# Fourier filter and two spectral MLP layers, float32: three tables of due steps and one choice of transposer are changed

## The chip, the cores and the metric

The kernel runs on one core of a Trainium2 chip. The metric is the device time of one execution in microseconds (us). TensorE is called PE in the rows (PEld is its weight load), VectorE DVE, ScalarE ACT, GpSimd POOL, and SyncE SP; SP only issues DMAs.

## The reference

Three layers follow each other on x of shape (4, 3136, 256), in float32. The first filters along the sequence; the other two are MLPs of width 1024, each behind a normalisation of its rows.

```python
def _attn_ref(x, filt_r, filt_i):
    X = np.fft.rfft(x, axis=1)
    return np.fft.irfft(X * (filt_r + 1j * filt_i)[None], n=x.shape[1], axis=1)

def _moe_ref(x, w_ch1, w_ch2):
    u = x + np.real(np.fft.fft(np.fft.fft(x, axis=1), axis=2))
    un = (u - mu(u)) / np.sqrt(var(u) + 1e-06)
    return u + np.maximum(un @ w_ch1, 0.0) @ w_ch2

def _moe2_ref(x, g_ln, w_ch1, w_ch2):
    xn = (x - mu(x)) / np.sqrt(var(x) + 1e-06) * g_ln
    return x + np.maximum(xn @ w_ch1, 0.0) @ w_ch2
```

## The kernel before

The sequence of 3136 = 64 x 49 is transformed as a two-dimensional DFT made of matmuls. For each of the four batches a first pass (`over_p`, a generator) goes over the factor 64 and a second (`over_q`) over the factor 49; the results go through DRAM. The rest works on 24 full **units** of 512 tokens (four tiles of 128), six for each batch, and on unit 24, the border of all batches, which has two tiles.

A unit is first prepared (`prep_ticks`: the mixing matmuls that make its tokens `u`, then its normalisation), then goes through the first MLP layer (`layer` 0, weights w1a and w2a) and later through the second (`layer` 1, w1b and w2b). Every layer of a unit is a block of eight **steps** m = 0 to 7, one for each 128 of the 1024 hidden columns. The blocks stand in the order (0,0), (1,0), (0,1), (2,0), (1,1), (3,0), and so on. With s the step at which block (U, 0) begins, (U-1, 1) begins at s+8, (U+1, 0) at s+16 and (U, 1) at s+24.

Each matrix product is done in three passes of a split operand, high times high, low times high and high times low, where high is the rounded value and low the remainder. A step is therefore `w1_step` (six matmuls `ps<-xth,w1` and `ps<-xtl,w1`, 512 columns each, line 766), `w1_evict` (ACT writes `hh`, line 776, then DVE writes `hl`, line 777) and `w2_step` (twelve matmuls of 256 columns, line 794). The main loop runs the first product two steps ahead:

```python
        for i, (U, layer, m) in enumerate(steps):
            if i + 2 < len(steps):
                w1_step(*steps[i + 2])
            for f in at.pop(i, []):
                f()
            if i in conv_at:
                run(cw, 1)
            w2_step(U, layer, m)
            if i + 2 < len(steps):
                w1_evict(*steps[i + 2])
```

All other work is cut into ticks (what a generator does up to its next `yield`), and tables of numbers say at which step, counted from s, each tick is issued (`at`). There is no scheduler: each engine runs its instructions in the order in which this program issues them. In a step an engine has the ticks first and the eviction of the hidden columns behind them.

The normalisation (`ln_ticks`) comes in two forms.
- For the blocks in the set `TURN` the tokens are turned without PE: a tick with the statistics (DVE, and a power on POOL), two ticks in which ACT writes two normalised tiles each (`xn`, line 654), a tick with a 32 x 32 transpose on DVE (line 668) and a DMA to DRAM (`xd`, line 670), a tick with four DMAs that bring it back turned (`xtl<-xd`, line 679), and two ticks that split it into `xth` (ACT, line 688 in layer 0 and 684 in layer 1) and `xtl` (DVE, lines 689 and 685).
- For the others a tick holds the statistics, the next the normalised tiles on DVE (line 663), and two ticks each transpose one half by PE (line 695) and split it from PSUM (lines 223 and 224 in layer 0, 697 and 698 in layer 1).

The pool of `xn` has one buffer. The second form is used in layer 0 by the first unit of each batch (6, 12, 18) and by the border unit 24. The title's "border unit" is any of these four: units that PE turns while the unit before them, U = 5, 11, 17 and 23, waits for its second layer. Their ticks are due at `PREPN`, s + 3, 3, 5, 7, 8, 9, 11, 13; the two PE transposes are the ticks at s+11 and s+13. The second layer of U has its ticks at `LNT`, s + 10, 11, 12, 13, 16, 19, 20, where the ticks at s+11 and s+12 write `xn`. In units whose layer 0 is in `TURN` the preparation has its ticks at `PREPT`.

The two passes of the next batches are ticks too. `over_p` lies over the end of a batch (around U = 5 and 11) and adds three matmuls of 512 columns to a step (line 220), an eviction (`gst`, line 370), an operand split on ACT and POOL (`sh`, `sl`, lines 223 and 224) and a load on SP (`xr<-in_x`, line 258). `over_q` lies over the other units of batches 0 to 2. From U = 17 on nothing but preparation and MLP is left.

Of the kernel before, what the change touches and what calls it, by code (L numbers as in the profile page):

```python
# [28 lines left out]
NU = 6 * B  # L29
# [108 lines left out]
OPQ = (2, 4)  # L138
MID = 16
PAIRS = [(4, 5), (10, 11), (0, 1), (2, 3), (12, 14), (6, 8)]  # L140
TURN = {(U, l) for U in range(3, NU) for l in range(2) if l or U % 6}
PREPT = (0, 1, 3, 4, 5, 6, 7, 8, 10, 13, 13)
LNT = (10, 11, 12, 13, 16, 19, 20)
PREP1 = (0, 1, 2, 3, 3, 4, 5, 5)
PREPS = (2, 3, 5, 8, 8, 9, 11, 11)
PREPN = (3, 3, 5, 7, 8, 9, 11, 13)
LN0 = (8, 10, 12, 12)
LN = (12, 13, 16, 19)
# [3 lines left out]
def spectral_mlp_kernel(ctx: ExitStack, tc, x, ff, cst, w1a, w2a, gln, w1b, w2b, out):  # L152
# [73 lines left out]
    def split_tiles(src, lo_eng=None):  # L226
        n = src.shape[0]
        h = spl.tile([128, 512], F32R, tag="h", name="sh")
        l = spl.tile([128, 512], F32R, tag="l", name="sl")
        w = 1  # L230
        for s in src.shape[1:]:
            w *= s
        flat = src.rearrange("p a d -> p (a d)") if len(src.shape) == 3 else src
        split(flat, h[:n, :w], l[:n, :w], lo_eng)
        return {"h": h, "l": l}
# [324 lines left out]
    def prep_ticks(U):  # L560
# [15 lines left out]
        if U:  # L576
            vs = [split_tiles(t, e) for t, e in zip(v_raw.pop(U), (nc.gpsimd, nc.gpsimd if (U, 0) in TURN else nc.vector))]
        else:
# [47 lines left out]
    def ln_ticks(U, layer, sets=None):  # L626
        n = tiles(U)
        u = u_of[U]
        xs = {}
        turn = (U, layer) in TURN  # L630
        xall = None
# [180 lines left out]
    with tc.manual_schedule():  # L812
# [98 lines left out]
        def put(s, it, k=1):  # L911
            at.setdefault(s, []).append(lambda: run(it, k))

        def call(s, f, *a):
            at.setdefault(s, []).append(lambda: f(*a))
# [5 lines left out]
        for U in range(NU + 1):  # L921
            s = index[U, 0]
            V = U + 1
            if V <= NU:
                it = prep_ticks(V)
                ws = PREPT if (V, 0) in TURN else (PREPS if V % 6 else PREPN) if U else PREP1
                for w in ws:
                    put(s + w, it)
                new = V % 6 == 0 and V < NU
                call((s - 3 if (V, 0) in TURN else s + 1 + new) if U else -1, load_v, V)  # L930
                if new:
                    ready[V // 6] = s + 2
            it = ln_ticks(U, 1)
            if U < NU:
                e = index[U + 1, 0]
                for w in [s + v for v in (LNT if (U, 1) in TURN else LN)] if U else [e - 8 + w for w in LN0]:
                    put(w, it)
            else:
                for w in (9, 10, 12, 13):
                    put(s + w, it)  # L940
# [54 lines left out]
def _launch(inputs):  # L995
# [44 lines left out]
    with tile.TileContext(nc) as tc:  # L1040
        spectral_mlp_kernel(tc, *args)
# [22 lines left out]
```

## Time and profile before

| | before |
|---|---|
| median of 3 runs | 1401.95 us (1398.85 to 1402.89) |
| profiled execution, its own time | 1401.71 us |
| span of its instructions | 1399.9 us, mean granted TensorE clock 0.992 |
| PE busy / weight load | 1358.1 us (97%) / 1198.6 us (86%) |
| DVE / ACT / POOL busy | 879.5 us (63%) / 748.2 us (53%) / 436.2 us (31%) |

The span runs from the first to the last instruction of the profiled execution; 1.8 us of its time lie around it. Times of rows are counted from the start of the span. PE is busy almost throughout, so time is lost where PE stands still, where its clock is lower, or where it is given more matmuls; the other engines matter where PE waits for them. A matmul's end is modelled and reaches past the start of the next, so PE's pace is read from the starts.

### The profile page before, as it was taken

The numbers are of one execution on the slowest core, as the hardware profiler recorded it, in microseconds if no ns is written. First come the engines' busy times: TensorE is split into PE (matmuls) and PEld (weight loads), VectorE is DVE, ScalarE is ACT, GpSimd is POOL, SyncE is SP. The second block draws the span as 40 slices with busy tenths as digits, with TensorE's granted clock in tenths as the row PEclk, the third lists the DMA queues.
The fourth block names the chain that finished last, engine by engine and source line by source line (L and its number), as shares of the span: only waits on it lengthen the run. The fifth ranks groups of instructions, "written<-read, shape, count | busy, mean of one in ns | idle before, by whom it ended". The sixth has DMA issues, their size and how long they took to land.

```text
span 1399.9 us, 23346 instructions
## 1 busy us (share of the span) xinstructions
PE 1358.1 (97%) x8611; PEld 1198.6 (86%) x8611; DVE 879.5 (63%) x1719; ACT 748.2 (53%) x1533; POOL 436.2 (31%) x379
## 2 busy tenths in 40 slices
PE   8979899999999999999999999999999999999988
PEld 6547798888888989898888998898898999999978
DVE  5978877777544766767444667677554554555433
ACT  5665555665535565756445656566534444454232
POOL 1746444544222333524033244344111101110000
PEclk9999999999999999999999999999999999999999
DMA  8872324363524634624525544444222413331210
GB/s 298 283 231 86 98 85 114 123 174 87 147 91 138 153 84 135 184 61 116 132 76 145 145 125 141 123 125 121 64 46 61 91 31 76 76 87 35 61 46 23
DMA packets 228642, 158.11 MB, mean 113 GB/s; under 512 B 168528, under 2 KB 192080, under 8 KB 228528
## 3 DMA queue, kind: packets, MB, share of 16 engines
q1 hardware_dynamic: 212576, 133.41, 34.9%
q10 hardware_dynamic: 15952, 23.20, 5.2%
q8 instruction: 68, 1.11, 0.3%
q14 instruction: 46, 0.38, 0.1%
HBM read 100.35 MB, written 56.23 MB: 112 GB/s over the span
## 4 chain that ended last, share of the span: by engine, by line
PE 85%; DVE 4%; ACT 4%; issue 2%; DMA 2%; SPq 1%; POOL 1%; ACTq 0%; DVEq 0%; POOLq 0%
PE ps L794 35%; PE ps L766 35%; PE ps L220 8%; PE ps L591 2%; ACT xn L654 2%; PE ps L308 1%; PE ps L325 1%; PE ps L478 1%; ACT hh L776 1%; DMA xr<-in_x 1%; DVE hl L777 1%; PE ps L446 1%; DVE wm L748 1%; DMA ww<-in_w2a 0%; PE ps L341 0%
## 5 line engine op out<-in xcount | busy, mean ns | idle before, releaser
L777 DVE SCALAR_TENSOR_TENSOR hl<-ps,hh 128x512 fp32r<-128x512 f32 (+1 forms) x400 | 270.2, 676 | 332.3 <-ACT hh L776 323.0
L776 ACT ACTIVATE hh<-ps 128x512 fp32r<-128x512 f32 (+1 forms) x400 | 234.1, 585 | 328.4 <-PE ps L794 318.5
L766 PE MATMUL ps<-xth,w1a 128*128 128x512 f32 (+1 forms) x800 | 247.0, 390 | 1.0 <-ACT xth L688 0.3
L766 PE MATMUL ps<-xth,w1b 128*128 128x512 f32 (+1 forms) x800 | 244.7, 388 | 0.0
L794 PEld LDWEIGHTS ps<-w2b,hh 128*128 128x128 f32 x1568 | 210.1, 190 | 24.7 <-ACT hh L776 11.6
L794 PE MATMUL ps<-w2b,hh 128*128 128x256 f32 x1568 | 218.8, 282 | 10.3 <-ACT hh L776 10.3
L794 PE MATMUL ps<-w2a,hh 128*128 128x256 f32 x1568 | 218.0, 281 | 3.7 <-ACT hh L776 3.3
L794 PEld LDWEIGHTS ps<-w2a,hh 128*128 128x128 f32 x1568 | 207.6, 189 | 15.5 <-ACT hh L776 4.1
L654 ACT ACTIVATE xn<-u,nb,rs 128x256 f32<-128x256 f32 x156 | 123.1, 838 | 70.3 <-DVE nb L647 47.4
L766 PE MATMUL ps<-xtl,w1a 128*128 128x512 f32 (+1 forms) x400 | 157.5, 394 | 1.8 <-DVE xtl L689 1.4
L766 PE MATMUL ps<-xtl,w1b 128*128 128x512 f32 (+1 forms) x400 | 156.2, 391 | 0.0
L643 POOL TENSOR_TENSOR rs<-rs,mhalf 128x4 f32<-128x4 f32 (+1 forms) x51 | 50.7, 994 | 334.0 <-DVE rs L642 220.5
L766 PEld LDWEIGHTS ps<-xth,w1a 128*128 128x128 f32 x800 | 136.9, 190 | 19.4 <-ACT xth L688 1.9
L766 PEld LDWEIGHTS ps<-xth,w1b 128*128 128x128 f32 x800 | 135.6, 188 | 16.7
L461 POOL TENSOR_TENSOR y<-y,t 128x512 f32<-128x512 f32 (+1 forms) x67 | 94.4, 1409 | 146.4 <-DVE t L459 113.8
L794 PE MATMUL ps<-w2a,hl 128*128 128x256 f32 x784 | 122.8, 278 | 4.0 <-DVE hl L777 3.9
L794 PE MATMUL ps<-w2b,hl 128*128 128x256 f32 x784 | 123.3, 279 | 0.0
L794 PEld LDWEIGHTS ps<-w2a,hl 128*128 128x128 f32 x784 | 104.4, 189 | 4.6 <-DVE hl L777 4.6
L224 POOL TENSOR_TENSOR sl<-gr,sh 98x512 fp32r<-98x512 f32 x48 | 62.2, 1295 | 146.3 <-ACT sh L223 146.3
L794 PEld LDWEIGHTS ps<-w2b,hl 128*128 128x128 f32 x784 | 105.1, 190 | 0.0
L798 DVE TENSOR_TENSOR u<-ps,u 128x512 f32<-128x512 f32 x98 | 63.2, 686 | 52.9 <-PE ps L794 52.9
L766 PEld LDWEIGHTS ps<-xtl,w1a 128*128 128x128 f32 x400 | 75.6, 189 | 20.6 <-DVE xtl L689 4.8
(130 smaller groups left out, 2074.8 us busy)
## 6 DMA issues: line engine op xcount, KB each, us to landing
fc<-in_ff SPq DMA_DIRECT2D x61, 512.0 KB
xd<-xn SPq DMA_DIRECT2D x39, 512.0 KB
xtl<-xd SPq DMA_DIRECT2D x156, 128.0 KB
vd<-vst ACTq DMA_DIRECT2D x64, 200.0 KB
xr<-in_x SPq DMA_DIRECT2D x48, 256.0 KB
vr<-vd SPq DMA_DIRECT2D x48, 256.0 KB
out<-u SPq DMA_DIRECT2D x24, 512.0 KB
gr<-gd SPq DMA_DIRECT2D x48, 196.0 KB
```

Source lines behind the costliest of these rows:

```text
L220: nc.tensor.matmul(out=o, lhsT=lhs[a], rhs=rhs[b], start=start and i == 0, stop=stop and i == 2)
L224: (lo_eng or nc.vector).tensor_tensor(out=lo, in0=src, in1=f32(hi), op=ALU.subtract)
L308: nc.tensor.matmul(out=o, lhsT=cf[i // 512][:k, i % 512:i % 512 + w], rhs=rhs[:k, c0:c1], start=start, stop=stop)
L461: (nc.gpsimd if b or t < n - 1 else nc.vector).tensor_tensor(out=y[:, :nk], in0=y[:, :nk], in1=t2[:, :nk], op=ALU.add)
L591: nc.tensor.matmul(out=o, lhsT=lhs, rhs=rhs[r], start=i == 0, stop=False)
L643: nc.gpsimd.tensor_tensor(out=rs[:, tl], in0=rs[:, tl], in1=mhalf[:, tl], op=ALU.pow)
L654: nc.scalar.activation(out=xs[t], in_=u[:, t].rearrange("p (k a j) -> p j k a", k=2, j=4), func=ACTF.Identity, scale=rs[:, t:t + 1], bias= ...
L766: nc.tensor.matmul(out=o, lhsT=w[:, a, k, m * 128:m * 128 + 128], rhs=xt[s][:, k, :n], start=i == 0, stop=i == 5)
L776: nc.scalar.activation(out=h[:, :n], in_=ps[:, :n], func=ACTF.Relu)
L777: nc.vector.scalar_tensor_tensor(out=l[:, :n], in0=ps[:, :n], scalar=0.0, in1=f32(h[:, :n]), op0=ALU.max, op1=ALU.subtract)
L794: nc.tensor.matmul(out=o[:, t % 2], lhsT=a[:, t * 128:t * 128 + 128], rhs=w[:, b, m], start=m == 0 and i == 0 and t % 2 == 0, stop=m == 7 ...
L798: nc.vector.tensor_tensor(out=u[:, t - 1:t + 1], in0=o, in1=u[:, t - 1:t + 1], op=ALU.add)
```

## The change

Four edits of the tables, lines 141 to 144 and 936 of the new kernel. Lines after 143 stand one lower in the new kernel (766 becomes 767).

```diff
-TURN = {(U, l) for U in range(3, NU) for l in range(2) if l or U % 6}
-PREPT = (0, 1, 3, 4, 5, 6, 7, 8, 10, 13, 13)
+TURN = {(U, l) for U in range(3, NU) for l in range(2) if (U < NU - 1 if l else U % 6)}
+PREPT = (0, 1, 3, 4, 5, 6, 7, 8, 10, 12, 12)
 LNT = (10, 11, 12, 13, 16, 19, 20)
+LNTN = (11, 14, 15, 16, 18, 20, 21)
...
-                for w in [s + v for v in (LNT if (U, 1) in TURN else LN)] if U else [e - 8 + w for w in LN0]:
+                for w in [s + v for v in ((LNT if (U + 1, 0) in TURN else LNTN) if (U, 1) in TURN else LN)] if U else [e - 8 + w for w in LN0]:
```

`LNTN` holds for U = 5, 11 and 17. The block (23, 1) leaves `TURN`: it takes the second form, at `LN`, s + 12, 13, 16, 19. The new `PREPT` holds for the 18 units of layer 0 that are in `TURN`.

**Unit 17, ACT.** ACT's instructions at steps s+10 to s+14, when unit 18 is turned by PE (`xth<-ps`) and the second layer of unit 17 is normalised (`xn`); before:

```order
L776 ACTIVATE hh<-ps 128x512 x4
L223 ACTIVATE xth<-ps 128x512
L654 ACTIVATE xn<-u,nb,rs 128x8x32 x2
L776 ACTIVATE hh<-ps 128x512
L654 ACTIVATE xn<-u,nb,rs 128x8x32 x2
L776 ACTIVATE hh<-ps 128x512
L223 ACTIVATE xth<-ps 128x512
L776 ACTIVATE hh<-ps 128x512 x3
```

And now:

```order
L777 ACTIVATE hh<-ps 128x512 x4
L224 ACTIVATE xth<-ps 128x512
L777 ACTIVATE hh<-ps 128x512 x2
L224 ACTIVATE xth<-ps 128x512
L777 ACTIVATE hh<-ps 128x512
L655 ACTIVATE xn<-u,nb,rs 128x8x32 x2
L777 ACTIVATE hh<-ps 128x512
L655 ACTIVATE xn<-u,nb,rs 128x8x32 x2
L777 ACTIVATE hh<-ps 128x512
```

The four writes of `xn` stood between the two halves of the border unit's `xth`, ahead of two evictions that PE needs; now they stand behind the second half. Units 5 and 11 move in the same way, with the work of `over_p` between.

**A unit of layer 0 in TURN, ACT.** ACT's instructions at steps s+11 to s+13 in a unit with work of `over_q` (`sh`, `vst`, `zt`); before:

```order
L654 ACTIVATE xn<-u,nb,rs 128x8x32 x2
L776 ACTIVATE hh<-ps 128x512
L223 ACTIVATE sh<-gr 98x512
L485 ACTIVATE vst<-ps 100x512
L489 ACTIVATE zt<-ps 128x4x49
L654 ACTIVATE xn<-u,nb,rs 128x8x32 x2
L776 ACTIVATE hh<-ps 128x512
L688 ACTIVATE xth<-xtl 128x512 x2
L776 ACTIVATE hh<-ps 128x512
```

And now:

```order
L655 ACTIVATE xn<-u,nb,rs 128x8x32 x2
L777 ACTIVATE hh<-ps 128x512
L224 ACTIVATE sh<-gr 98x512
L486 ACTIVATE vst<-ps 100x512
L490 ACTIVATE zt<-ps 128x4x49
L689 ACTIVATE xth<-xtl 128x512 x2
L655 ACTIVATE xn<-u,nb,rs 128x8x32 x2
L777 ACTIVATE hh<-ps 128x512 x2
```

The split of layer 0's operand went from behind the second pair of `xn` and an eviction to ahead of them. DVE's two `xtl` move with it.

**Block (24, 0), PE.** PE's matmuls in one of the half-width steps of the border unit (256 columns in the first product); before:

```order
L766 MATMUL ps<-xth,w1a 128x256 x2
L766 MATMUL ps<-xtl,w1a 128x256
L794 MATMUL ps<-w2a,hh 128x256 x4
L794 MATMUL ps<-w2a,hl 128x256 x2
L766 MATMUL ps<-xth,w1a 128x256 x2
```

And now:

```order
L767 MATMUL ps<-xth,w1a 128x256 x2
L767 MATMUL ps<-xtl,w1a 128x256
L696 MATMUL ps<-ctail,xn 128x128 x4
L795 MATMUL ps<-w2a,hh 128x256 x4
L795 MATMUL ps<-w2a,hl 128x256 x2
```

Four transposes of unit 23's second layer are new here, and four more three steps later; its five DMAs through DRAM, its DVE transpose and its four `xn` on ACT are gone, and four `xn` on DVE take the place of the last.

## Rows read from the trace of the kernel before

**Rows 1.** The page, part 1: busy us (share of span) x instructions.

```profile
PE 1358.1 (97%) x8611; PEld 1198.6 (86%) x8611; DVE 879.5 (63%) x1719; ACT 748.2 (53%) x1533; POOL 436.2 (31%) x379
```

**Rows 2.** Who waited for whom, PE: total us, times, longest us.

```profile
PE ps L794 <- ACT hh L776: 13.5, 7, 3.0
...
PE ps L766 <- DVE xtl L689: 1.4, 5, 0.3
```

**Rows 3.** The same for ACT.

```profile
ACT xn L654 <- PE ps L695: 22.8, 4, 6.0
```

**Rows 4.** Order of time, PE, unit 5: start, us, instruction [idle before <-releaser].

```profile
406.33 0.40 PE L220 MATMUL ps<-sl,chi 128*128 128x512 f32 x1
409.72 2.08 PE L794 MATMUL ps<-w2b,hh 128*128 128x256 f32 x8 [3.00 <-ACT hh L776]
```

**Rows 5.** The same, PE, units 11, 17 and 23.

```profile
733.16 0.40 PE L220 MATMUL ps<-sl,chi 128*128 128x512 f32 x1
736.56 0.86 PE L794 MATMUL ps<-w2b,hh 128*128 128x256 f32 x4 [3.00 <-ACT hh L776]
...
1054.06 0.60 PE L695 MATMUL ps<-ctail,xn 128*128 128x128 f32 x4
1056.79 0.62 PE L794 MATMUL ps<-w2b,hh 128*128 128x256 f32 x3 [2.13 <-ACT hh L776]
...
1340.40 0.38 PE L695 MATMUL ps<-ctail,xn 128*128 128x128 f32 x2
1342.92 1.20 PE L794 MATMUL ps<-w2b,hh 128*128 128x256 f32 x8 [2.13 <-ACT hh L776]
...
1344.40 0.39 PE L766 MATMUL ps<-xth,w1a 128*128 128x256 f32 x2
...
1346.17 1.10 PE L794 MATMUL ps<-w2b,hh 128*128 128x256 f32 x8
```

**Rows 6.** Stretches: us, busy us of five engines, granted clock, DMA share, GB/s.

```profile
409.40:412.80 3.40, 3.08 (x13) 3.06 (x14) 1.82 (x3) 3.40 (x7) 0.17 (x2) 0.51 0.23 77
736.50:740.40 3.90, 3.84 (x16) 3.55 (x17) 2.60 (x4) 3.45 (x7) 0.86 (x1) 0.57 0.17 59
1057.90:1061.30 3.40, 3.40 (x12) 2.82 (x12) 2.55 (x4) 1.77 (x4) 0.00 (x0) 0.50 0.00 0
```

**Rows 7.** Order of time, PE and ACT, block (24, 0).

```profile
1357.25 0.28 PE L766 MATMUL ps<-xtl,w1a 128*128 128x256 f32 x1
1359.58 0.74 PE L794 MATMUL ps<-w2a,hh 128*128 128x256 f32 x4 [2.05 <-ACT hh L776]
...
1358.54 0.72 ACT L684 ACTIVATE xth<-xtl,g_sb 128x512 fp32r<-128x512 f32 x1 [4.29 <-DMA xtl<-xd]
```

**Rows 8.** The same, PE and ACT, unit 5 some steps later.

```profile
420.64 0.40 PE L766 MATMUL ps<-xtl,w1a 128*128 128x512 f32 x1
...
423.01 0.40 PE L794 MATMUL ps<-w2a,hh 128*128 128x256 f32 x2
...
420.64 0.63 ACT L223 ACTIVATE sh<-xr 128x512 fp32r<-128x512 f32 x1 [6.41 <-DMA xr<-in_x]
```

**Rows 9.** The same, PE: a unit with `over_q`, then a late unit without.

```profile
844.78 0.62 PE L794 MATMUL ps<-w2b,hl 128*128 128x256 f32 x4
...
847.49 0.75 PE L794 MATMUL ps<-w2b,hh 128*128 128x256 f32 x5
...
1150.98 0.62 PE L766 MATMUL ps<-xth,w1b 128*128 128x512 f32 x2
...
1152.36 1.10 PE L794 MATMUL ps<-w2b,hh 128*128 128x256 f32 x8
```

**Rows 10.** The same, ACT, the same two units.

```profile
844.28 0.60 ACT L776 ACTIVATE hh<-ps 128x512 fp32r<-128x512 f32 x1
...
1148.85 1.58 ACT L654 ACTIVATE xn<-u,nb,rs 128x256 f32<-128x256 f32 x2
```

**Rows 11.** A stretch of the late unit, columns as in Rows 6.

```profile
1148.90:1150.20 1.30, 1.30 (x10) 1.16 (x9) 0.69 (x1) 1.30 (x3) 0.00 (x0) 1.00 0.00 0
```

## Prediction

> **What bounds the kernel now.** I read the page first: PE is busy 1358.1 of 1399.9 us [rows 1], so the kernel is as long as PE's matmuls plus the time in which PE stands still or runs slowly. The list of waits then says who stops PE. The largest entry by far is the second product waiting for ACT's `hh`: 13.5 us in only seven waits, up to 3.0 us each [rows 2]. ACT has an entry of four that fits it: `xn` waits for PE's transposes, 22.8 us in four, up to 6.0 us [rows 3]. The order of time shows how the two belong together. In unit 5 PE has nothing to do from the end of the matmul at 406.33 until 409.72, and what it waits for is `hh` [rows 4]; the same happens in units 11, 17 and 23 [rows 5]. It is a knot in the issue order. The single `xn` buffer is still being read by the border unit's second half, whose transposes PE runs at step s+13; the write of `xn` for the second layer, due at s+11, stands on ACT ahead of the evictions that PE needs before and after that step. ACT waits for PE, and once the transposes are through, PE waits for ACT.
>
> The granted clock adds to it. Just behind the stalls of units 5, 11 and 17 stretches of about 3.4 us have a mean clock of 0.51, 0.57 and 0.50, that is the lower level, 1.2 of 2.4 GHz [rows 6]; before them PE had stood still for 2 to 3 us.
>
> **The change, part by part.** Pace first: six matmuls of 512 columns take 1152.36 - 1150.98 = 1.38 us, 0.23 each [rows 9]; 256 columns are taken as half, 0.115 (an estimate from that); two more transposes lengthen a group from 0.38 to 0.60 us, 0.11 each [rows 5].
>
> *A, the stalls.* Behind the new order of ticks `xn` is written at s+14 or later, when the transposes of s+13 have run and the evictions in between have been made. What goes, start to start less the matmuls that start in between: unit 5 409.72 - 406.33 - 0.23 = 3.16 [rows 4]; unit 11 3.40 - 0.23 = 3.17; unit 17 2.73 - 0.44 = 2.29; unit 23 2.52 - 0.22 = 2.30 [rows 5]. Unit 23's second layer has another: ACT sits 4.29 us on the DMA that brings its turned tokens, because in the border block a step is only half as long, and PE stands still for 1359.58 - 1357.25 - 0.12 = 2.21 us [rows 7]. That layer no longer goes through DRAM. Sum 13.1 us, which agrees with the 13.5 us of all seven waits.
>
> *B, the clock.* Without the stall there is nothing ahead of these stretches that differs from the stretches beside them, which run at 1.00. At half speed half of the time is lost: 0.49 of 3.08 busy us, 0.43 of 3.84 and 0.50 of 3.40 [rows 6], together 1.5 + 1.65 + 1.7 = 4.85 us.
>
> *C, what trails the stalls.* In unit 5 SP is held by the DMA of the late turned tokens, loads of `over_p` behind it come late, ACT waits 6.41 us for one, and PE takes 2.37 us from 420.64 to 423.01 for four matmuls worth 0.92 [rows 8]: 1.45 us. In the new order these loads stand ahead of that DMA. In unit 23 ACT has still to catch up, and six half-width matmuls take 1346.17 - 1344.40 = 1.77 instead of 0.69 us [rows 5]: 1.1 us. Sum 2.5 us.
>
> *D, the first-layer splits.* PE waits five times for `xtl` of line 689 [rows 2]; each stands in a unit with `over_q`, where ACT is full in steps s+11 to s+13, and I count a sixth that waits for `xth`. In the one shown, the four matmuls from 844.78 and the six behind them take until 847.49, 2.71 us, against 4 x 0.115 + 1.38 = 1.84 [rows 9]: 0.87 us lost, six times 5.2 us. The splits now come ahead of a pair of `xn` and an eviction. Two obstacles. (1) The eviction behind them comes later: ACT's `hh` at 844.28 [rows 10] is pushed by two splits of about 0.6 us, to 845.5, done at 846.1. PE needs it at 847.49 less the 0.87 it no longer loses, 846.6: it holds, by 0.5 us. This edit is costed at nothing because of that half microsecond; without it up to 5.2 us come back. (2) The turned tokens must have landed. In units with `over_q` they have for microseconds; in late units ACT is free for the split at 1148.85 [rows 10], and the DMA engines fall silent at 1148.90 [rows 11]. ACT may wait a little. Its `hh` would be ready at about 1148.9 + 1.2 + 1.6 + 0.6 = 1152.3, and PE needs it one step behind the second product at 1152.36, so at 1152.36 + 2.76 = 1155.1: 2.8 us to spare. So the late units neither gain nor lose.
>
> *E, what is added.* Eight transposes of 128 columns on PE: 8 x 0.11 = 0.9 us. The Trainium skill, "TensorE: Matmul & The Clock Gate", Part 4 (PE-mode transpose), gives about 275 ns for one 128 x 128 transpose within a kernel. As eight times that the term would be 2.2 us and the sum 1.3 us smaller. The rows speak for the smaller price: a second and third pair stretch a group by 0.22 us. The four `xn` on DVE and the evictions of the transposes lie beside PE; DVE and ACT have gaps in each half-width step.
>
> *F, the new places.* For units 5, 11 and 17 the chain from the DVE transpose to the split shrinks from six steps (s+13 to s+19) to four (s+16 to s+20), about 11 to 14 us. The trace does not show these steps with the chain there. Behind a waiting split on ACT stand the evictions of hidden columns. The bounds are nothing, and the row of the one split that did wait for its DMA, 2.2 us of PE [rows 7] with a stretch of slow clock of 1.6 behind it, three times 3.8 = 11.4 us. I take nothing: in those steps the next unit's mixing makes the steps longer than in the half-width block of that row, and SP now has its other loads behind it. POOL only exchanges a power and a split.
>
> Sum: 13.1 + 4.85 + 2.5 + 5.2 - 0.9 = 24.75 us. The profiled execution would fall from 1401.7 to 1376.9 (span 1375.1); against the median of the runs, 0.25 us higher, 1377.
>
> **The rivals.**
>
> *The splits give nothing (D falls out).* The lateness passes from `xtl` to the eviction behind it. For it: only 0.5 us of margin, and DVE's `hl` has to follow as well. Against it: the same margin at each of these units. Time 1377 + 5.2 = 1382.
>
> *The stall is handed on (F at its upper bound).* The splits of units 5, 11 and 17 wait for their DMA at s+20, as the one in block (24, 0) did [rows 7]. For it: two steps fewer for the same two transfers. Against it: those steps are twice as long as there. Time 1377 + 11.4 = 1388.
>
> *The change doesn't do what it says.* ACT or DVE still meets the `xn` buffer before it is free, or the first half of the transposes waits instead, so that A, B and C stay but for unit 23: 1395 to 1400. Against it: in the new order both halves of `xth` stand ahead of the first `xn`.
>
> *Slower: the splits at s+12 wait for the turned tokens in all 18 units.* The place is ACT's first split, the price one microsecond of PE for each microsecond by which `hh` misses its use. It decides from the landing on: it must come over 2.8 us later than at 1148.90 to cost anything in a late unit, and some 4.3 us later in every unit to eat the 25 us. At 5 us later, 18 x 2.2 = 40 us, the time is 1417. Against it: no DMA but the turned tokens' own runs at that place in late units [rows 11].
>
> **How the numbers follow.** The forecast, 1377 with its own range of 1373 to 1381 (a few tenths at places that I did not sum, such as unit 11's loads, and small waits of the new order), has 0.70. D falling out has 0.11, the stall handed on in full or in part 0.12, no effect 0.04, slower 0.02, more gain than summed 0.01. The range 1373 to 1387 holds the forecast, the loss of D and most of the partial hand-on, about 0.85. The runs of this kernel lie within 4 us, 0.3%, and that is about what a measurement can tell from no change. Faster by over 0.3% (below 1397.7) comes to 0.95, within 0.3% to 0.03, slower to 0.02.
>
> **What the new profile would show.** If A is right, PE's waits for `hh` fall from 13.5 to about 1 us, and ACT's entry of `xn` behind the transposes is gone. If B is right, no stretch at the lower clock is left in the three places. If C is right, ACT's long waits for `xr<-in_x` at unit 5 are gone. If D is right, PE's waits for `xtl` of the first layer are gone, and the ten matmuls take 1.84 us. If E is right, eight more transposes appear near the end at 0.11 us. What would make me wrong: a wait of ACT's splits on `xtl<-xd` in units 5, 11 and 17 or at s+12, or waits of PE for `hh` or `hl` in the units with `over_q`.

## The result, and the profile after

The changed kernel takes 1378.09 us (median of 4 runs, 1374.3 to 1378.42), the kernel before beside it 1400.41 us (4 runs). The ratio is 0.9833, with a 95% interval of 0.9808 to 0.9858, so it is 1.7% faster. The profiled execution took 1378.22 us, with a span of 1376.4 us and a mean granted clock of 0.996. Against the profiled execution before that is 1401.71 - 1378.22 = 23.5 us; the prediction had summed 24.75 us. One execution of the kernel before that stood beside the first four experiments took 2731.68 us; it is left out of their ratios.

The first row of the page answers to [rows 1]. PE has eight more matmuls, and 9.0 us less busy time. About 4.85 us of that is the lower clock behind three stalls, by the working of term B; what the rest consists of was not read.

```profile
PE 1349.1 (98%) x8619; PEld 1195.2 (87%) x8619; DVE 890.1 (65%) x1721; ACT 746.0 (54%) x1529; POOL 441.2 (32%) x379
```

The list of PE's waits in the changed kernel (total us, times, longest us) answers to [rows 2]:

```profile
PE ps L795 <- DVE hl L778: 4.2, 3, 2.0
...
PE ps L767 <- DVE xtl L690: 2.0, 5, 0.4
...
PE ps L795 <- ACT hh L777: 1.2, 2, 0.7
```

The wait for `hh` fell from 13.5 to 1.2 us, and ACT's entry of [rows 3], `xn` behind the transposes, is gone. The wait for `xtl`, which the fourth term of the prediction meant to remove, is not gone. It rose from 1.4 to 2.0 us, and this the prediction did not foresee. The 1.2 us for `hh` are two waits in the first two blocks, which the kernel before had too; so only five of the seven waits of [rows 2], 12.3 of the 13.5 us, were those of term A. The prediction took all seven as a check of its 13.1 us.

Unit 5 in order of time, PE, at the place of [rows 4]:

```profile
404.74 0.60 PE L696 MATMUL ps<-ctail,xn 128*128 128x128 f32 x4
405.09 0.48 PE L221 MATMUL ps<-sh,chi 128*128 128x512 f32 x1
405.41 0.39 PE L221 MATMUL ps<-sh,clo 128*128 128x512 f32 x1
405.64 0.40 PE L221 MATMUL ps<-sl,chi 128*128 128x512 f32 x1
405.87 1.08 PE L795 MATMUL ps<-w2b,hh 128*128 128x256 f32 x8
```

The second product starts 0.23 us behind the matmul ahead of it, where it had started 3.39 us behind. The stretches that begin with this product in units 5, 11 and 17 answer to [rows 6] (us; busy us of PE, PEld, DVE, ACT, POOL; granted clock; DMA share; GB/s):

```profile
405.80:409.20 3.40, 3.40 (x23) 3.01 (x22) 1.45 (x3) 2.07 (x5) 1.29 (x1) 1.00 0.35 124
725.30:729.20 3.90, 3.90 (x26) 3.47 (x25) 1.45 (x3) 2.57 (x5) 1.29 (x1) 1.00 0.32 114
1040.10:1043.50 3.40, 3.40 (x26) 3.14 (x24) 1.45 (x3) 1.86 (x3) 0.00 (x0) 1.00 0.00 0
```

The clock is 1.00, the higher level (2.4 GHz), where it had been 0.50 to 0.57, and PE starts 23 to 26 matmuls instead of 12 to 16 in the same time. On ACT the load that came 6.41 us late in unit 5 [rows 8] is there when it is wanted. ACT's entry in the list of waits before, and the same split now in order of time, which shows no wait:

```profile
ACT sh L223 <- DMA xr<-in_x: 16.3, 4, 6.4
```

```profile
410.38 0.62 ACT L224 ACTIVATE sh<-xr 128x512 fp32r<-128x512 f32 x1
```

None of these four waits for a load of `xr` is left in the list of the changed kernel.

To see where the time came from, the kernel is cut at the last update of `u` of each block (DVE, line 798 before, 799 after; it is issued right behind the block's last matmul). Each number below is the start of that update less the start of the one that ends the block in front, or the sum over the blocks named.

```
blocks              before   after   difference
(2,1) + (3,1)        51.42   50.23     -1.19
(4,1) + (6,0)        61.67   55.03     -6.64   unit 5
(6,1) + (7,1)        52.52   52.01     -0.51
(10,1) + (12,0)      60.61   55.03     -5.58   unit 11
(16,1)               26.98   23.06     -3.92   unit 17
(17,0) to (22,0), each block       0.00   late units
(22,1)               24.66   21.18     -3.48   unit 23
(24,0)               14.88   13.11     -1.77   unit 23, DMA
```

The late units repeat to a hundredth of a microsecond, so differences of a few tenths in such a table can be read. There are two exceptions. Blocks that hold the stalls of units 5, 11 and 23 differ by 0.7 to 2 us between executions (the last section comes back to it). And the first blocks differ: the ends of (0,0) and (0,1) lie up to 3 us apart between executions in which nothing there was changed, and are left out of what follows.

### The profile page after: what moved, and what is told of

It is laid out like the page before. It is cut to its first block, busy times and chain, and to the rows that moved or that the text cites. A ratio compares the mean times of both kernels' runs of the same rounds, so it can differ in the third digit from the quotient of the medians.

```text
span 1376.4 us, 23356 instructions
## 1 busy us (share of the span) xinstructions
PE 1349.1 (98%) x8619; PEld 1195.2 (87%) x8619; DVE 890.1 (65%) x1721; ACT 746.0 (54%) x1529; POOL 441.2 (32%) x379
## 4 chain that ended last, share of the span: by engine, by line
PE 87%; DVE 6%; ACT 2%; issue 2%; DMA 1%; POOL 1%; SPq 0%; ACTq 0%; DVEq 0%; POOLq 0%
PE ps L795 36%; PE ps L767 35%; PE ps L221 8%; PE ps L592 2%; PE ps L309 2%; DVE t L460 1%; PE ps L326 1%; DVE xtl L690 1%; PE ps L479 1%; PE ps L447 1%; DVE y L455 1%; DVE hl L778 1%; DVE wm L749 1%; PE ps L696 1%; PE ps L342 0%
## 5 line engine op out<-in xcount | busy, mean ns | idle before, releaser
L767 PEld LDWEIGHTS ps<-xth,w1b 128*128 128x128 f32 x800 | 135.7, 189 | 16.6
L655 ACT ACTIVATE xn<-u,nb,rs 128x256 f32<-128x256 f32 x152 | 120.0, 838 | 51.8 <-DVE nb L648 51.8
L462 POOL TENSOR_TENSOR y<-y,t 128x512 f32<-128x512 f32 (+1 forms) x67 | 98.8, 1475 | 145.7 <-DVE t L460 114.0
```

The costliest lines, as they stand in the source:

```text
L462: (nc.gpsimd if b or t < n - 1 else nc.vector).tensor_tensor(out=y[:, :nk], in0=y[:, :nk], in1=t2[:, :nk], op=ALU.add)
L655: nc.scalar.activation(out=xs[t], in_=u[:, t].rearrange("p (k a j) -> p j k a", k=2, j=4), func=ACTF.Identity, scale=rs[:, t:t + 1], bias= ...
L767: nc.tensor.matmul(out=o, lhsT=w[:, a, k, m * 128:m * 128 + 128], rhs=xt[s][:, k, :n], start=i == 0, stop=i == 5)
```

## The experiments

The theory: ACT's `xn`, held by the single buffer, is the knot; what the four places lost (the stall, the lower clock behind it, and what trails it) goes with it, whichever way the knot is undone; and the splits (the prediction's term D) give less than forecast because DVE, not ACT, is what is late now. The rivals: the lower clock or the trailing work has a cause of its own; the splits gave their 5.2 us and something else lost them; the DMA stall of (24, 0) was only a tail of the stall before it.

### e1_order, e2_turn, e3_splits: the three parts alone

Each takes one part of the change into the kernel before.

```diff
# e1_order
+LNTN = (11, 14, 15, 16, 18, 20, 21)
+ ... ((LNTN if U in (5, 11, 17) else LNT) if (U, 1) in TURN else LN) ...
# e2_turn
+TURN = {... if (U < NU - 1 if l else U % 6)}
# e3_splits
+PREPT = (0, 1, 3, 4, 5, 6, 7, 8, 10, 12, 12)
```

> Only the new order of ticks (LNTN) for units 5, 11 and 17; the rest as before. By the theory (stall, clock behind it and what trails it all come from ACT's xn standing ahead of evictions) the time falls by what the blocks around these units lost in the comparison of before and after: 6.6 + 5.6 + 3.9 = 16.1 us, to about 1384 to 1386, and no stretch at the lower clock is left there. Rival (the low clock has another cause than the stall): only the bare stalls go, 3.16 + 3.17 + 2.29 = 8.6 us, and the three stretches at the lower clock stay. PE's waits for hh fall from 13.5 to about 5 us (unit 23 keeps its two).

> Only the block (23, 1) out of TURN; units 5, 11, 17 and the splits as before. By the theory unit 23's stall, what trails it and the DMA stall go, less eight transposes: by the blocks of before and after 3.5 + 1.8 = 5.25 us, by the prediction's terms 2.30 + 1.1 + 2.21 - 0.9 = 4.7 us. Rival (the added transposes and evictions eat it): under 2 us.

> Only the first-layer splits a step sooner (PREPT 12, 12). The prediction has 5.2 us for it. By the blocks of before and after it is 2.4 us at most, because DVE, not ACT, is late: its xtl takes up to 1.2 us instead of 0.64 while POOL works. PE's waits for xtl stay, some 0.4 us each. Rival (the prediction's term is right and the rest of the shortfall lies elsewhere): 5 us less and no wait of PE for xtl.

Measured: e1_order 1387.08 us, ratio 0.9900 (0.9882 to 0.9919); e2_turn 1394.58 us, 0.9956 (0.9939 to 0.9973); e3_splits 1400.61 us, 0.9992 (0.9981 to 1.0003). With the 1402.6 us of the kernel before in these runs that is 14.0 (11.4 to 16.6), 6.2 and 1.1 us. The same cut into blocks, with e4_buffer of the next part:

```
blocks            before   e1_order  e2_turn  e3_splits  e4_buffer   after
(2,1) + (3,1)      51.42     51.43     51.51     50.21      51.50     50.23
(4,1) + (6,0)      61.67     55.03     60.98     61.09      61.49     55.03
(6,1) + (7,1)      52.52     52.60     52.54     52.02      52.57     52.01
(10,1) + (12,0)    60.61     55.03     61.43     61.69      60.76     55.03
(16,1)             26.98     23.06     26.98     26.99      23.06     23.06
(22,1)             24.66     25.13     21.18     25.12      21.18     21.18
(24,0)             14.88     16.27     13.11     16.42      16.01     13.11
```

Each part does its work where it stands; elsewhere the larger differences lie in blocks that still hold a stall. In e1_order the blocks of units 5, 11 and 17 are as long as in the changed kernel, 16.1 us less. The mean granted clock is 1.00 in ten microseconds around each of the three places (402 to 412, 722 to 732 and 1036 to 1046 us). Clock and trailing work went with the stall, and the rival of 8.6 us falls. The timed 14.0 us agrees with 16.1 only within its interval. Unit 23 took 1.9 us more in this execution than in the profile of before (the section on the hardware comes back to it); whether that is the rest of the difference is not shown. In e2_turn the two blocks of unit 23 give 3.48 + 1.77 = 5.25 us. In e3_splits the splits give 1.2 + 0.5 us in the four blocks shown, and the timed 1.1 us (-0.4 to 2.7) excludes the prediction's 5.2. PE's waits, first for `hh` in e1_order and e2_turn, then for `xtl` in e3_splits:

```profile
PE ps L795 <- ACT hh L777: 4.8, 3, 2.1
```

```profile
PE ps L794 <- ACT hh L776: 9.5, 5, 3.0
```

```profile
PE ps L766 <- DVE xtl L689: 2.0, 5, 0.4
```

Of the 13.5 us of [rows 2] the first part takes 8.7 and the second 4.0, and the third leaves PE's wait for `xtl` in place, a little longer than before.

### e4_buffer: the knot undone without moving anything

```diff
+            if layer and U in (17, 23):
+                xall = xall or fp.tile([128, 4 * D], F32, tag="f", name="xn")
             xall = xall or xnp.tile([128, 4 * D], F32, tag="xn", name="xn")
```

> Nothing is moved: before, but the second layers of units 17 and 23 write xn into another pool's buffer, which nothing uses at that time. If the single buffer is the knot, xn no longer waits for PE there, the stalls of units 17 and 23 go with the slow clock behind the first, and the time falls by 3.9 + 3.5 = 7.4 us; the DMA stall of (24, 0) and units 5 and 11 stay. Rival (it is the work of four xn ahead of the evictions, 0.8 us each, whatever the buffer): PE still waits for hh in both units, and less than 3 us is won.

Measured: 1393.1 us, ratio 0.9944 (0.9927 to 0.9960), which is 7.9 us of 1402.6. Blocks (16,1) and (22,1) are exactly as long as in the changed kernel, 23.06 and 21.18 us, although every instruction stands where it stood before. So in these two units it was the buffer; for units 5 and 11 a second buffer was not tried. Four `xn` ahead of an eviction cost PE nothing; what cost was that they could not begin. The row of PE behind the transposes of unit 17, in order of time, shows no wait, where [rows 5] had 2.13 us:

```profile
1051.47 0.60 PE L697 MATMUL ps<-ctail,xn 128*128 128x128 f32 x4
1051.83 1.19 PE L796 MATMUL ps<-w2b,hh 128*128 128x256 f32 x8
```

The stretch that begins there, columns as in [rows 6], is at the higher clock, where it had been 0.50:

```profile
1052.00:1055.40 3.40, 3.40 (x25) 3.14 (x24) 2.70 (x4) 1.19 (x2) 0.00 (x0) 1.00 0.00 0
```

### e9_turn23: would later ticks have served unit 23 too?

```diff
-TURN = {... if (U < NU - 1 if l else U % 6)}
+TURN = {... if l or U % 6}
```

> The changed kernel, but the second layer of unit 23 stays in TURN and only gets the later ticks of LNTN, as units 5, 11 and 17 did. If the reorder alone cures the stall, block (22, 1) takes as long as in the changed kernel. The DMA wait must then stay: the chain from the DVE transpose to the split lies in steps half as wide, so ACT waits for xtl<-xd and PE for hh; block (24, 0) takes 2 to 6 us longer than the 13.1 us of the changed kernel, and the time is that much over 1378. Rival (the DMA stall was only the tail of the first stall): (24, 0) takes 13 us, and without eight transposes the time is 0.9 us lower than the changed kernel's.

Measured: 1382.02 us, ratio 0.9866 (0.9845 to 0.9888). Block (22,1) takes 21.18 us, as in the changed kernel, and (24,0) takes 19.26 instead of 13.11, 6.15 us more, just above the 2 to 6 us expected. (Between the profiles the whole is only 3.8 us longer, since the first blocks happened to be shorter in this one.) ACT and PE in order of time:

```profile
1338.26 0.72 ACT L685 ACTIVATE xth<-xtl,g_sb 128x512 fp32r<-128x512 f32 x1 [6.75 <-DMA xtl<-xd]
```

```profile
1339.03 1.22 PE L767 MATMUL ps<-xth,w1b 128*128 128x512 f32 x2 [4.92 <-ACT xth L685]
```

The split waits 6.75 us for the turned tokens and PE 4.92 us for the split. The DMA stall is a cost of its own: it also stays in e4_buffer, where the first stall is gone and (24,0) takes 16.01 us. In half-width steps later ticks make it worse. Of the ways tried, only taking (23, 1) out of `TURN` removes both.

### e8_probe: DVE beside POOL, measured by itself

Behind the last step of the changed kernel stands a row of operations whose results go nowhere: four subtractions on DVE alone (line 1003), then four adds on POOL (line 1007) and eight subtractions on DVE (line 1009) that start together.

```diff
+        w = 512
+        for src in (ta[:, :w], ps):
+            for i in range(4):
+                nc.vector.tensor_tensor(out=ta[:, w:], in0=src, in1=ta[:, :w], op=ALU.subtract)
...
+            for i in range(4):
+                nc.gpsimd.tensor_tensor(out=tb[:, w:], in0=tb[:, :w], in1=tb[:, :w], op=ALU.add)
+            for i in range(8):
+                nc.vector.tensor_tensor(out=ta[:, :w], in0=src, in1=ta[:, :w], op=ALU.subtract)
```

> The changed kernel with a row of adds and subtractions behind its last step, which leave the output alone: DVE alone, 128x512 from SBUF; the same with POOL's adds at the same time; then both again with DVE reading one operand from PSUM. Theory (DVE and POOL slow each other on SBUF): a subtraction from SBUF takes about 0.64 us alone and 1.1 to 1.3 us beside POOL, one with a PSUM operand is slowed less, POOL's add takes longer beside DVE. Rival (no contention; the long xtl had a wait in it): the same time alone and beside POOL.

The groups of the profile, each asked for in the stretch in which it stands (count | busy us, mean ns). First with both operands of DVE in SBUF, DVE alone, then DVE and POOL beside each other:

```profile
L1003 DVE TENSOR_TENSOR ta<-ta 128x512 f32<-128x512 f32 x4 | 2.8, 688 | 0.1
...
L1009 DVE TENSOR_TENSOR ta<-ta 128x512 f32<-128x512 f32 x4 | 5.6, 1410 | 0.1
...
L1007 POOL TENSOR_TENSOR tb<-tb 128x512 f32<-128x512 f32 x4 | 5.5, 1379 | 0.5 <-DVE ta L1005 0.3
```

Then the same with one operand of DVE in PSUM:

```profile
L1003 DVE TENSOR_TENSOR ta<-ps,ta 128x512 f32<-128x512 f32 x4 | 2.8, 691 | 0.1
...
L1009 DVE TENSOR_TENSOR ta<-ps,ta 128x512 f32<-128x512 f32 x6 | 4.1, 689 | 0.2
...
L1007 POOL TENSOR_TENSOR tb<-tb 128x512 f32<-128x512 f32 x4 | 4.2, 1038 | 0.5 <-DVE ta L1005 0.3
```

A subtraction with two operands in SBUF takes 0.69 us alone and 1.41 us beside POOL's adds, and POOL's adds, which take 1.04 us beside subtractions with an operand in PSUM, take 1.38 us beside those from SBUF. With one operand in PSUM DVE keeps its time alone (0.69 us). These adds by themselves were not run, so that POOL loses nothing there is not shown. The theory holds, and more sharply than expected: for DVE the operand in PSUM takes the cost away altogether.

### e6_first and e7_ydve: two ways to part DVE and POOL

e5_after is the changed kernel again, as the measure for the two. e6_first issues the two split ticks at s+12 ahead of the `over_q` tick of that step; e7_ydve leaves the order and gives POOL's add of `y` to DVE.

```diff
# e6_first
-                for w in ws:
+                for w in ws if (V, 0) not in TURN else ws[:-2]:
                     put(s + w, it)
+                if (V, 0) in TURN:
+                    late += [(s + w, it) for w in ws[-2:]]
...
+        for w, it in late:
+            first(w, it)
# e7_ydve
-                (nc.gpsimd if b or t < n - 1 else nc.vector).tensor_tensor(
+                nc.vector.tensor_tensor(
                     out=y[:, :nk], in0=y[:, :nk], in1=t2[:, :nk], op=ALU.add)
```

> The changed kernel once more, so that the two runs beside it have their own measure on the same chip: 22 to 24 us under before, five waits of PE for xtl with 2.0 us in all.

> The changed kernel with the two splits of each unit in TURN issued ahead of over_q's tick at the step s+12, so that DVE makes xtl before y and t, and POOL adds y behind them. Late units are as in the changed kernel. Theory (xtl is slow because POOL adds y at the same time): xtl takes about 0.64 us each in the units with over_q, PE's five waits for it go, the ten matmuls take 1.84 us, and 2 to 3 us of the prediction's 5.2 come back: some 0.4 to 0.7 us in each of five or six blocks. Rival (ACT's split or the landing of the turned tokens is late): the waits for xtl stay and the blocks take as long as now.

> The changed kernel with over_q's add of y on DVE instead of POOL; xtl stays behind y and t on DVE and now behind the add too. Theory (it is POOL's work beside it that slows xtl): xtl takes about 0.64 us each again, though it starts later by the add (0.64 us or less); the ten matmuls lose less than now. Rival (DVE's own length is the cause, POOL does nothing): xtl stays at 1.2 us each and PE waits longer by the add, 0.6 us in each of five places.

Measured on one chip: e5_after 1378.16 us, ratio to before 0.9829 (0.9815 to 0.9844); e6_first 1373.40 us, 0.9793 (0.9778 to 0.9808); e7_ydve 1381.15 us, 0.9852 (0.9836 to 0.9869). What this is about, in the unit whose step was read in the profile of before: the DVE split and POOL's add in order of time, first in the changed kernel,

```profile
885.28 2.40 DVE L690 TENSOR_TENSOR xtl<-xtl,xth 128x512 fp32r<-128x512 f32 x2
...
885.39 1.74 POOL L462 TENSOR_TENSOR y<-y,t 128x512 f32<-128x512 f32 x1 [0.97 <-DVE t L460]
```

then in e6_first, and in e7_ydve:

```profile
876.82 1.28 DVE L690 TENSOR_TENSOR xtl<-xtl,xth 128x512 fp32r<-128x512 f32 x2
```

```profile
888.52 0.69 DVE L462 TENSOR_TENSOR y<-y,t 128x512 f32<-128x512 f32 x1
889.13 1.29 DVE L690 TENSOR_TENSOR xtl<-xtl,xth 128x512 fp32r<-128x512 f32 x2
```

Both edits bring the pair of `xtl` back from 2.40 to 1.28 us, so POOL's add beside it was the cause of its length, as in the probe. But only one of them is a gain. The pair is also late. In the changed kernel and in e7_ydve it stands on DVE behind `y` and `t`; in e7_ydve the add comes on top, PE waits 0.58 us where it had waited 0.43, and other waits on DVE grow (PE's for `z` from 2.6 to 5.1 us in all). In e6_first the split starts as soon as ACT has made `xth`. The ten matmuls in this unit, PE in order of time, in the changed kernel and in e6_first:

```profile
885.55 0.62 PE L795 MATMUL ps<-w2b,hl 128*128 128x256 f32 x4
...
887.74 0.50 PE L767 MATMUL ps<-xtl,w1a 128*128 128x512 f32 x1 [0.43 <-DVE xtl L690]
888.08 0.40 PE L795 MATMUL ps<-w2b,hh 128*128 128x256 f32 x2
```

```profile
876.45 0.62 PE L795 MATMUL ps<-w2b,hl 128*128 128x256 f32 x4
...
878.28 0.40 PE L795 MATMUL ps<-w2b,hh 128*128 128x256 f32 x2
```

That is 2.53 us and 1.83 us, against 2.71 before [rows 9] and an ideal of 1.84. e6_first is the fastest kernel of this study, 4.8 us under the changed kernel; 3.9 us of it lie in the blocks behind (0,1), all in units with `over_q`.

### e10_sooner: the splits one more step sooner

```diff
-PREPT = (0, 1, 3, 4, 5, 6, 7, 8, 10, 12, 12)
+PREPT = (0, 1, 3, 4, 5, 6, 7, 8, 10, 11, 11)
```

> The changed kernel with the first-layer splits another step sooner (PREPT 11, 11). In units with over_q xtl then comes before y and t of the step s+12, and the gain of e6_first should show, about 0.6 us in each of six blocks. In late units ACT's split waits for the turned tokens with one or two evictions behind it; by the prediction's margin of 2.8 us, less the 2.76 us of a step, nothing is left, so that PE waits for hh between 0 and 1.5 us in each of some ten units: between 1374 and 1390. Rival (the tokens land early enough): no wait for hh in late units, 1374.

Measured: 1376.42 us, ratio 0.9824 (0.9801 to 0.9848). The blocks of e5_after to e10_sooner side by side:

```
blocks            e5_after  e6_first  e7_ydve  e9_turn23  e10_sooner
(2,1) + (3,1)       50.23     49.54     49.74     50.23       49.65
(6,1) + (7,1)       52.01     50.70     51.90     52.02       50.70
(12,1) + (13,1)     52.01     50.70     51.87     52.03       50.70
(18,1)              22.08     22.08     22.08     22.08       23.27
(20,1)              22.08     22.08     22.08     22.08       23.06
(24,0)              13.11     13.11     13.11     19.26       13.11
```

The units with `over_q` gain as in e6_first. And yet in all five places where PE waited for `xtl` the pair takes 2.38 or 2.39 us again; in the one shown it runs beside another of POOL's instructions. DVE and POOL in order of time:

```profile
872.75 2.39 DVE L690 TENSOR_TENSOR xtl<-xtl,xth 128x512 fp32r<-128x512 f32 x2
...
872.85 1.74 POOL L225 TENSOR_TENSOR sl<-y,sh 128x512 fp32r<-128x512 f32 x1
```

So a long pair costs PE nothing if it starts early enough; in the changed kernel it was both late and long. What lateness alone would cost is not shown, since e7_ydve puts the add itself ahead of the pair.

There is a price: the late units lose 0.3 to 1.2 us each, 3.8 us over all of them. In these ACT's split waits for the turned tokens with an eviction behind it, and PE waits for that eviction; ACT and PE in order of time:

```profile
1124.37 1.15 ACT L689 ACTIVATE xth<-xtl 128x512 fp32r<-128x512 f32 x2 [3.35 <-DMA xtl<-xd]
```

```profile
1128.54 1.21 PE L795 MATMUL ps<-w2b,hh 128*128 128x256 f32 x8 [0.81 <-ACT hh L777]
```

So the margin of 2.8 us that the prediction gave these units at s+12 was about right: one step of 2.76 us uses it up.

## Why the prediction was right, and where a term was off

The measured 1378.09 us lie in the forecast's own range, 1373 to 1381.

*A, B and C, the stalls with the clock and what trails them: right.* They were summed by unit as 3.16 + 1.5 + 1.45 = 6.1 us for unit 5, 3.17 + 1.65 = 4.8 for unit 11, 2.29 + 1.7 = 4.0 for unit 17 and 2.30 + 2.21 + 1.1 - 0.9 = 4.7 for unit 23 (E with it). The blocks gave 6.6, 5.6, 3.9 and 5.25, together 21.4 against 19.6 us. A large part of the difference lies where the prediction had not summed. Behind the stall of unit 11 there is trailing work too, and in unit 5 it goes on one step past the 423.01 at which the prediction stopped; PE in the kernel before, in order of time:

```profile
423.63 0.97 PE L794 MATMUL ps<-w2a,hh 128*128 128x256 f32 x6 [0.21 <-DVE hl L777]
...
748.13 0.40 PE L220 MATMUL ps<-sh,clo 128*128 128x512 f32 x1
...
749.36 0.97 PE L794 MATMUL ps<-w2a,hh 128*128 128x256 f32 x6 [0.20 <-DVE hl L777]
```

In unit 5 two matmuls worth 0.23 us take 0.62, from 423.01 to 423.63. In unit 11 four worth 0.69 take 1.23. That is 0.4 and 0.5 of the missing 0.5 and 0.8 us; the 0.55 us of unit 23 are not traced. That the clock of units 5, 11 and 17 hangs on the stall is shown by e1_order, for unit 17 also by e4_buffer, in which no instruction was moved.

*D, the splits: the direction was right, the size was not.* The term was 5.2 us. Over the blocks up to (15,1) the changed kernel won about 2.1 us with it, and alone it gave 1.1 us (-0.4 to 2.7). Place by place, (3,1) won 0.89 us, the whole forecast; it is the sixth place, whose `xth` had been late. The five whose `xtl` had been late won only 0.25 to 0.31 us each. Three other blocks won 0.4 us together, and in (1,1) and (3,0) the new place cost 0.6 us. The step that failed is the sentence that put PE's wait for `xtl` down to ACT, which is full, and then asked only whether the eviction and the landing would hold. ACT's eviction and the landing held. What was not asked is what stands ahead of `xtl` on DVE, and what runs beside it. In (3,1) nothing does: DVE waits for ACT, and the pair takes 1.29 us. In (1,1) the long pair pushes DVE's later work back, and PE waits for `hl`, one of the signs of being wrong that the prediction had named. DVE in (3,1), then PE in (1,1), in the changed kernel:

```profile
352.18 1.29 DVE L690 TENSOR_TENSOR xtl<-xtl,xth 128x512 fp32r<-128x512 f32 x2 [0.53 <-ACT xth L689]
```

```profile
244.42 0.72 PE L795 MATMUL ps<-w2b,hl 128*128 128x256 f32 x4 [0.32 <-DVE hl L778]
```

In the five others `y` and `t` of `over_q` stand ahead at s+12, and POOL's add of `y`, which follows them, then runs at the same time as the split. The second `xtl` of a pair took up to 1.8 us instead of 0.69. The Trainium skill has this: "SBUF — State Buffer", section "SBUF: two separate sides", says that VectorE and GpSimd share one pair of ports: of a VectorE instruction with two SBUF inputs and a GpSimd instruction that reads SBUF, the one that starts first holds the pair for the whole instruction and the other waits. The probe agrees in which operand matters (1.41 us with both in SBUF, 0.69 us with one in PSUM), and the two engines' starts take turns there, one subtraction to one add in each 1.44 us (5.75 us for four). In "whole" the probe leaves something open: 1.44 us is less than the recorded 0.69 + 1.04 = 1.73 us one behind the other, so some part of these lengths does not keep the other engine out. Which part, no run here shows. What D could have given, 0.87 us at each of six places, was read rightly from the rows: with the order of e6_first the six blocks (2,1), (3,1), (6,1), (7,1), (12,1) and (13,1) are 0.88 to 1.00 us shorter than before. e10_sooner gives the same six blocks within 0.12 us with the pair still long in five of them, so an earlier place in DVE's queue was enough.

*E, eight transposes: right.* In block (24, 0) a step with four of them and the next without, PE in order of time:

```profile
1328.07 0.40 PE L767 MATMUL ps<-xth,w1a 128*128 128x256 f32 x2
...
1328.78 0.60 PE L696 MATMUL ps<-ctail,xn 128*128 128x128 f32 x4
1329.13 0.72 PE L795 MATMUL ps<-w2a,hh 128*128 128x256 f32 x4
...
1329.92 0.40 PE L767 MATMUL ps<-xth,w1a 128*128 128x256 f32 x2
...
1331.32 0.39 PE L767 MATMUL ps<-xth,w1a 128*128 128x256 f32 x2
```

The step with them takes 1.85 us and the one without 1.40, so four cost 0.45 and eight 0.9 us, as forecast. One transpose is recorded with 0.27 us, but the four start 0.11 us apart. The prediction spoke of a second and a third pair; [rows 5] show one more pair for the 0.22 us, which is 0.11 for each transpose as summed.

*F, nothing for the new places: right.* In units 5, 11 and 17 no split of the second layer waited for its DMA. In the list of ACT's waits of the changed kernel all splits of a second layer together waited once:

```profile
ACT xth L685 <- DMA xtl<-xd: 1.4, 1, 1.4
```

This one is of unit 7, whose ticks are as before, at 530.00 us; PE shows no wait there, and the kernel before has the same wait with 1.7 us. e9_turn23 shows what the rival's price would have been in steps half as long, 6.15 us.

The terms together: 21.4 instead of 19.6, and 2.1 instead of 5.2, which makes 23.5 instead of 24.75 us. Two misses of opposite sign helped the total.

## What to carry to other kernels

When an engine waits for a buffer that another engine frees later in the program, look for what stands behind the waiting instruction; a second buffer or a later place for the write cures the same stall (e4_buffer and e1_order gave the same block (16,1)). The later place needs no memory and cost nothing in units 5, 11 and 17, but 6 us in the half-width steps of unit 23 (e9_turn23). Before a step is moved on one engine, read the queue of the next engine in its chain as well, and what a third engine does at that moment. A wait named after a tile says which engine was last, not which was slow: ask what it would wait for if the named one came in time.

## What was not expected of the hardware

DVE and POOL slow each other when both read only SBUF. A 128x512 subtraction in float32 takes 0.69 us alone and 1.41 us beside POOL's adds, and 0.69 us beside them when one of its operands lies in PSUM. POOL's add takes 1.38 us beside the first kind of subtraction and 1.04 us beside the second (e8_probe).

The granted clock does not always fall behind the same stall. In unit 23 PE waited 2.13 us in the execution of before [rows 5] and as long in e1_order, whose code is the same there. The same stretch behind the stall, before and in e1_order:

```profile
1342.90:1347.40 4.50, 3.95 (x29) 3.55 (x30) 3.22 (x5) 2.77 (x6) 0.00 (x0) 1.00 0.00 0
```

```profile
1324.50:1329.00 4.50, 4.48 (x25) 4.49 (x26) 3.21 (x5) 2.69 (x5) 0.00 (x0) 0.62 0.00 0
```

The clock was 1.00 in one and 0.62 in the other, and the two blocks of unit 23 together took 39.54 us before and 41.40 in e1_order. The two blocks of unit 11, (10,1) and (12,0), took 60.61 to 61.69 us in the four executions that still had its stall, and 55.03 us in all seven that did not. Unit 17's stall, 2.13 us like that of unit 23, gave no such spread: block (16,1) took 26.98 or 26.99 us in the three executions that had it. A kernel without the stall is spared this spread too. What decides it no run here shows.
